# Shift filter as phase-by-channel contractions with keys turned on chip, gate sum from normalised rows, cross products ahead of the other spectral products

## The chip, the cores and the metric

The kernel runs on one core of one Trainium2 chip. The metric is the device time of one execution in microseconds (us), and a median over several executions is quoted. The profiled span is about 2 us shorter than the measured time.

The core has TensorE (PE, matrix products; PEld is its weight load), VectorE (DVE), ScalarE (ACT), GpSimd (POOL) and SyncE (SP, which issues DMAs). Each engine works through its own list of instructions in order; semaphores make one engine wait for another. A tile is a buffer in on-chip memory; PSUM tiles are here those that TensorE writes and ScalarE evicts.

## The reference, cut to what matters

```python
x = A_q                                             # 2048 rows of 640
g = sigmoid((x * gate_w).sum(-1, keepdims=True))    # one gate value per row
# branch A
k_shift = sum(k_pad[:, t:t+S, :] * shift_k[:, 3-t] for t in range(4))   # 4-tap causal filter per channel
kv = k_shift * v
y = irfft(rfft(kv, 2S) * rfft(ssm_k, 2S))[:S] + kv * ssm_D
a = q * y
# branch B
h = layernorm(x)
u = gelu(h^T @ w1 + b1);  b = (u @ w2 + b2)^T
out = g * a + (1 - g) * b
```

## The kernel before: the parts that matter

The long convolution is done as a discrete transform. TensorE multiplies by a 128x128 factor (`FTB`), VectorE combines the four phases ("mixing") and multiplies spectra, and TensorE transforms back. The 2048 rows come in four blocks of 512; partition i of a block holds rows 4i to 4i+3, one for each of four phases.

No order of instructions is written down. A list scheduler, run when the kernel is built, gives each engine its order from modelled durations. An operation with a smaller `prio` goes first among those that are ready. And where a later user of a PSUM tile (here GELU) has a hazard, the scheduler moves it onto the first matmul of that tile:

```python
                for d in deps:                      # hazards of the operation that reads the PSUM tile
                    if d.vt is not vt:
                        if d not in vt.first.deps:
                            vt.first.deps.add(d)    # ... now hold back the tile's first matmul
```

The first-layer matmuls of branch B have the last priority, so they fill what the rest leaves of TensorE:

```python
                mms(vt, items, prio=10 ** 6 + 4 * ft + hk, name="m1")
            g_ = act(GT[:, ft, :]..., two, ACT.Gelu_apprx_tanh, bias=..., vt=vt, prio=0, name="gelu")
```

The keys are transposed by DMA, 128 channels at a time. The filter multiplies strided columns of the transposed keys by diagonal matrices, seven matmuls for each group of 128 channels and each row block; ScalarE evicts, and VectorE multiplies by the values:

```python
                tt("DVE", DG[...], ident, shkf, ALU.mult)      # 20 diagonal matrices, once
        def kv(hk):
            # ... (cut)
                    for q in range(4):
                        items.append((s[512*b + 128*q : 512*b + 512], V(KT[h], base + q, [[4, 128]]), DG[:, db, 0:4 - q, :], ...))
                    for q in range(1, 4):
                        items.append((s[512*b : 512*b + 128*q], V(KT[h], base - 4 + q, [[4, 128]]), DG[:, db, 4 - q:4, :], ...))
                act(o, ..., ACT.Copy, vt=vt, name="kve")
            tt("DVE", o, kb[:, :, :], vi, ALU.mult, prio=0)    # kv = shifted keys times values
        for hk in range(2):
            kv(hk)                                             # first pair: vkv
        # first kv transform, mixing
        for hk in range(2, 4):
            kv(hk)                                             # second pair: kv
        # second kv transform, mixing
```

The gate sum is one VectorE instruction with accumulator for each of 16 row tiles, beside the row statistics. The spectral products come after both transforms:

```python
            stt("DVE", junk[1][:, :], xs, 1.0, gwb[:, :], ALU.mult, ALU.mult, acc=gpre[:, t:t + 1])
        # ... (cut)
        def y1(g):
            product(A1[g], A1[g], V0[g])
            product(V1[g], A0[g], V1[g])     # the cross product
            acc_dma(A1[g], V1[g])            # sum of both, by an accumulating DMA
```

## Time and profile before

| | before |
|---|---|
| median time | 203.06 us (202.98 to 203.24) |
| profiled span | 201.0 us |
| TensorE busy | 187.1 us, 93% |
| VectorE busy | 183.4 us, 91% |
| filter matmuls | 140 |

The timeline of TensorE before, 40 to 76 us: start, duration, engine, line, operation, tiles, count, and in brackets the idle just before with what ended it.

```profile
40.04 8.88 PE L293 MATMUL pp<-DG,KT 128*128 128x512 bf16 x70
...
51.44 1.25 PE L293 MATMUL pp<-X,ring 128*128 128x320 bf16 x8
52.53 9.39 PE L293 MATMUL pp<-vkv,FTB 128*128 128x320 bf16 x64
61.89 7.13 PE L293 MATMUL pp<-DG,KT 128*128 128x512 bf16 x56
68.86 3.42 PE L293 MATMUL pp<-X,ring 128*128 128x320 bf16 x24
72.12 0.43 PE L293 MATMUL pp<-kv,FTB 128*128 128x320 bf16 x2
73.91 2.08 PE L293 MATMUL pp<-kv,FTB 128*128 128x320 bf16 x14 [1.36 <-DVE kv L611]
```

Here `DG,KT` is the filter, `vkv,FTB` and `kv,FTB` are the first and second kv transform, and `X,ring` is the first layer, the filler. TensorE is nearly full while VectorE works towards the kv products; eight filler matmuls stand just ahead of the first transform.

The chain of waits of before, where it changes engine:

```profile
72.37 1.50 DVE kv L611
...
73.91 124.00 PE pp L293 x910
```

The last VectorE piece is the second product of the second pair.

### The profile page before, as it was taken

The numbers are of one execution on the slowest core, as the hardware profiler recorded it, in microseconds if no ns is written. First come the engines' busy times: TensorE is split into PE (matmuls) and PEld (weight loads), VectorE is DVE, ScalarE is ACT, GpSimd is POOL, SyncE is SP. The second block draws the span as 40 slices with busy tenths as digits, with TensorE's granted clock in tenths as the row PEclk, the third lists the DMA queues.
The fourth block names the chain that finished last, engine by engine and source line by source line (L and its number), as shares of the span: only waits on it lengthen the run. The fifth ranks groups of instructions, "written<-read, shape, count | busy, mean of one in ns | idle before, by whom it ended". The sixth has DMA issues, their size and how long they took to land.

```text
span 201.0 us, 3282 instructions
## 1 busy us (share of the span) xinstructions
PE 187.1 (93%) x1383; PEld 136.2 (68%) x1383; DVE 183.4 (91%) x204; ACT 102.9 (51%) x145; POOL 24.8 (12%) x24
## 2 busy tenths in 40 slices
PE   0769989999999979999999999999999999999993
PEld 0456656576656747777777777788888887688672
DVE  7799979998997999999999999999999982899672
ACT  4798899965698658841111221131313136631762
POOL 1002245403033060000000005003100000000000
PEclk9999999999999999999999999999999999999999
DMA  5999999999940000007501805995999900311033
GB/s 158 344 406 348 284 160 201 305 344 231 221 176 0 0 3 0 0 3 234 183 0 34 273 10 103 160 360 218 166 273 341 359 14 0 130 68 65 0 138 126
DMA packets 35226, 32.37 MB, mean 161 GB/s; under 512 B 15618, under 2 KB 32652, under 8 KB 35212
## 3 DMA queue, kind: packets, MB, share of 16 engines
q1 hardware_dynamic: 34080, 29.53, 49.2%
q0 software_dynamic: 1088, 2.62, 8.1%
q8 instruction: 11, 0.18, 0.4%
q14 instruction: 3, 0.02, 0.0%
q10 hardware_dynamic: 44, 0.01, 0.0%
HBM read 23.25 MB, written 2.62 MB: 129 GB/s over the span
## 4 chain that ended last, share of the span: by engine, by line
PE 62%; DVE 25%; POOL 5%; DMA 4%; issue 2%; SPq 1%; ACT 0%
PE pp L293 62%; DVE stats L825 5%; DVE junk L629 5%; DVE C L611 5%; DMA gwb<-in_gate_w_dram 4%; POOL vtmp L621 3%; DVE X L622 3%; DVE SS L611 3%; POOL rstd L611 2%; DVE kv L611 1%; DVE vkv L611 1%; DVE mv L827 1%; SPq L267 1%; ACT O L649 0%; DVE O L611 0%
## 5 line engine op out<-in xcount | busy, mean ns | idle before, releaser
L293 PE MATMUL pp<-X,ring 128*128 128x320 bf16 x384 | 53.6, 299 | 0.0
L293 PE MATMUL pp<-GT,W 128*128 128x320 bf16 x384 | 52.8, 299 | 0.0
L293 PEld LDWEIGHTS pp<-GT,W 128*128 128x128 bf16 x384 | 43.4, 113 | 8.9 <-issue 0.2
L611 DVE TENSOR_TENSOR C<-C 128x2560 bf16<-128x2560 bf16 (+1 forms) x28 | 49.0, 1769 | 0.3
L293 PEld LDWEIGHTS pp<-X,ring 128*128 128x128 bf16 x384 | 37.5, 98 | 14.5
L649 ACT ACTIVATE C<-pp 128x640 bf16<-128x640 f32 x64 | 39.3, 752 | 7.1 <-PE pp L293 7.0
L649 ACT ACTIVATE O<-pp,c,omg 128x640 bf16<-128x640 f32 (+1 forms) x17 | 14.5, 853 | 36.7 <-PE pp L293 36.7
L649 ACT ACTIVATE GT<-pp,cc 128x640 bf16<-128x640 f32 x12 | 9.5, 793 | 33.7 <-PE pp L293 33.7
L611 DVE TENSOR_TENSOR tm<-C,C 128x5120 bf16<-128x5120 bf16 x8 | 22.2, 2817 | 0.0
L293 PE MATMUL pp<-wT,FTB 128*128 128x320 bf16 x128 | 19.8, 314 | 0.0
L293 PE MATMUL pp<-DG,KT 128*128 128x256 bf16 (+3 forms) x140 | 18.1, 288 | 0.6 <-DMA KT<-in_A_k_dram 0.6
L611 DVE TENSOR_TENSOR C<-tm 128x2560 bf16<-128x2560 bf16 x12 | 17.4, 1484 | 0.1
L293 PEld LDWEIGHTS pp<-DG,KT 128*128 128x128 bf16 x140 | 13.1, 115 | 5.5 <-DMA KT<-in_A_k_dram 1.2
L293 PEld LDWEIGHTS pp<-wT,FTB 128*128 128x128 bf16 x128 | 11.8, 102 | 7.4 <-ACT C L649 2.5
L649 ACT ACTIVATE cgb<-pp,gg 128x640 bf16<-128x640 f32 x16 | 12.7, 793 | 5.7 <-PE pp L293 5.7
L293 PE MATMUL pp<-ident,ssm 128*128 128x128 bf16 x80 | 8.8, 266 | 6.9 <-DMA ssm<-in_A_ssm_k_dram 5.6
L825 DVE BATCH_NORM_STATS2 stats<-X 128x6 f32<-128x320 bf16 x32 | 13.7, 464 | 1.2 <-DMA X<-in_A_q_dram 1.2
L649 ACT ACTIVATE ksh<-pp 128x1024 bf16<-128x1024 f32 (+1 forms) x12 | 10.1, 879 | 8.2 <-PE pp L293 8.2
L293 PE MATMUL pp<-C,GTB 128*128 128x320 bf16 x96 | 13.6, 299 | 0.0
L629 DVE SCALAR_TENSOR_TENSOR junk<-X,gwb 128x640 bf16<-128x640 bf16 x16 | 12.9, 803 | 0.2 <-DMA gwb<-in_gate_w_dram 0.2
L262 POOL DMA_DIRECT2D C<-C x4 | 5.1, 1506 | 61.1 <-DVE C L611 61.1
L293 PEld LDWEIGHTS pp<-ident,ssm 128*128 128x128 bf16 x80 | 6.3, 128 | 9.2 <-DMA ssm<-in_A_ssm_k_dram 5.6
(49 smaller groups left out, 163.1 us busy)
## 6 DMA issues: line engine op xcount, KB each, us to landing
ring<-in_B_w_dram SPq DMA_DIRECT2D x12, 512.0 KB, 8.5
W<-in_B_w_dram SPq DMA_DIRECT2D x8, 768.0 KB, 7.8
ssm<-in_A_ssm_k_dram SPq DMA_DIRECT2D x4, 640.0 KB, 9.0
X<-in_A_q_dram SPq DMA_DIRECT2D x4, 640.0 KB, 9.2
C<-C POOLq DMA_DIRECT2D x4, 640.0 KB, 9.1
out_dram<-O SPq DMA_DIRECT2D x7, 320.0 KB, 2.4
vkv<-in_A_v_dram SPq DMA_DIRECT2D x2, 640.0 KB, 5.0
v<-in_A_v_dram SPq DMA_DIRECT2D x2, 640.0 KB, 6.3
```

Source lines behind the costliest of these rows:

```text
L262: ins = engobj.dma_start(out_ap, in_ap, accum_op=ALU.add, max_dma_last_dim=2560)
L267: ins = engobj.dma_start(out_ap, in_ap)
L293: ins = self.nc.tensor.matmul(ps_ap, lhsT=lhsT, rhs=rhs, start=start, stop=stop, skip_group_check=True)
L611: return SC.add(eng, d, lambda s: T.op(eng, lambda e: e.tensor_tensor(o, a, b, op), [a, b], [o]), [a, b], [o], prio=prio, name="tt")
L621: return e.tensor_scalar(o, a, s1, None, op0=op0)
L622: return e.tensor_scalar(o, a, s1, s2, op0=op0, op1=op1)
L629: eng, lambda e: e.scalar_tensor_tensor(out=o, in0=a, scalar=sc, in1=b, op0=op0, op1=op1, accum_out=acc),
L649: return T.op("ACT", lambda e: e.activation(o, src, func, **kw), rr + [src], ww)
L825: SC.add("DVE", 0.46, (lambda o, i: lambda s: T.op("DVE", lambda e: e.bn_stats(o, i), [i], [o]))(o, i), [i], [o])
L827: SC.add("DVE", 0.2, (lambda o, i: lambda s: T.op("DVE", lambda e: e.bn_aggr(o, i), [i], [o]))(o, i), [i], [o])
```

## The change

The intent is to relieve TensorE and VectorE in the first 74 us.

- **Filter.** VectorE permutes natural key rows (`kn` to `kp`), and a DMA turns them so that a column holds 4 phases by 32 channels. One matmul contracts those 128 values at once; a second one, shifted by a column, adds the taps that reach into the four rows before. 140 matmuls become 160 narrower ones. The filter matrix `KF` is built by two GpSimd products.
- **Gate.** With the row normalised already, the sum is that of the normalised row times `gate_w`, scaled back by the row's deviation, plus the mean times the sum of `gate_w`. VectorE multiplies later (8 wider products), ScalarE sums, and GpSimd combines 16 numbers per partition.
- **Cross product.** It goes ahead of the other products, in halves, so that it can start before the second mixing.

```diff
+        kn = [alloc(f"kn{i}", [128, 4, D], BF16, at=base_of(ring[1]) + 5120 * i) for i in range(2)]
+        kp = [alloc("kp0", ..., at=base_of(ring[1]) + 10240), alloc("kp1", [128, NG, 128], BF16, at=base_of(GT))]
...
-        def kT_load(h, db):
-            dma(KT[h][:, db, 16:1040], A_k[...], transpose=True, chain=True)
+        def k_turn(hk):
+            o, i = kp[hk % 2], kn[hk % 2]
+            ... tensor_copy(ov, iv) on VectorE
+            dma(KT[hk // 2][:, :, c0:c0 + 128], o[:, :, :], transpose=True, chain=True)
...
-            stt("DVE", junk[1][:, :], xs, 1.0, gwb[:, :], ALU.mult, ALU.mult, acc=gpre[:, t:t + 1])
...
-                tt("DVE", DG[...], ident, shkf, ALU.mult, mode=1)
+                for g0 in (0, 10):
+                    tt("POOL", KF[:, g0:g0 + 10, :, :], cw taps, m32 mask, ALU.mult)
+                for hk in range(2):
+                    k_turn(hk)
...
+                    items.append((s[128*b : 128*b + 128], KT[h][:, g, c0:c0 + 128], KF[:, g, 0:4, :], True, False))
+                    items.append((s[128*b : 128*b + 96], KT[h][:, g, c0 - 1:c0 + 127], KF[:, g, 4:7, :], False, True))
...
+            if ft in (1, 3, 5, 7):
+                    tt("DVE", gb[:, :, :], X[...], gwb, ALU.mult)
+                        act(junk[:, :], gb[:, b, :], ACT.Copy, acc=gacc[:, t:t + 1], name="gsum")
+        tt("POOL", gth, vtmp, rstd);  tt("POOL", gth, gth, gacc)
+        ts("POOL", gpre, mv mean, gws);  tt("POOL", gpre, gpre, gth)
+        act(gth[:, :], gpre[:, :], ACT.Tanh, scale=0.5)
...
         def y1(g):
             product(A1[g], A1[g], V0[g])
-            product(V1[g], A0[g], V1[g])
...
+        cross(0)
+        cross(1)
         y1(0)
```

## The prediction

> **What bounds it now.** The chain of waits falls in two. From 9 to 73.9 us it is almost all VectorE (statistics, gate sums, mixings, kv products), with some GpSimd; from 73.9 to 197.9 us it is TensorE alone, 910 matmuls (busy by stretch: 123.98 of 124.10 us). So the time is T, the end of the second kv product, plus about 127 us that only fewer matmuls after T shorten. Before T, TensorE is busy 60 of 65 us, partly with filler (48 first-layer matmuls).
>
> **What changes (groups and timeline of before).**
> - Filter: 140 matmuls, 17.4 us of TensorE, become 160 of 128 or 96 columns. The 128-column transposes, each with new weights, follow one another every 55 ns or so (five in 0.31 us of weight loads), so I estimate 8.5 to 9 us. ScalarE then limits: a 1024-column eviction takes 0.92 us, so a quarter of the filter needs 2.3 us. All of it lies before T.
> - VectorE loses 16 gate products (0.80 us each with the accumulator read: 12.9 us) and the 2.77 us diagonal build. It gains eight 1280-column products (0.74 us each, after T, where it has room) and four key permutations, estimated 0.85 us each, before T. Net before T: about 12 us less.
> - GpSimd gains two 128x2240 products for the filter matrix. The Trainium skill, "GPSIMD Engine Reference", section 3.1, gives 4497 ns for 2048 elements; scaled, an estimate of 4.9 us each. No run yet shows it.
>
> **Critical path.** Adding up the changed order with durations of before (the same sum puts before at 201 us of span, T at 73.6): the filter ends near 43 us, against 52.5; but the first transform of kv waits for VectorE, which reaches the kv products only at 47 to 54 us. No filler stands there, so TensorE idles 4 to 8 us: most of its saved 9 us. The value-mixing operations now stand ahead of the second pair of kv products. The second filter-matrix product comes when VectorE runs two-input operations. The skill, "SBUF — State Buffer", section "Who interferes with whom", says these and a GpSimd read exclude each other; before agrees in part (a GpSimd scaling of 4 elements took 2.69 us beside one long VectorE operation, 0.24 us elsewhere). If VectorE loses about 5 us there, directly or by waiting for the row scale queued behind it, T is about 74 us; if not, 70 us. After T there are 8 matmuls more (1.1 us).
>
> **Time.** Span 198.7 to 205; the measured time is 2 us above the span. I predict 202.3 us, range 197.5 to 207: faster by over 2% 0.2, within 2% 0.67, slower by over 2% 0.13. The large TensorE saving buys nearly nothing.
>
> **What would show each step.**
> - TensorE busy about 178 us instead of 187, with one idle of 4 us or more before the first kv transform, ended by a VectorE product.
> - Filter matmuls about 9 us in all, paced by ScalarE evictions.
> - VectorE at about 178 us busy; about 5 us lost near 20 to 40 us, beside the second GpSimd filter-matrix product.
> - The chain: VectorE until about 74 us, then TensorE unbroken.
>
> **What would make it wrong.** Permutations at half the assumed rate (T about 2.5 us later), or GpSimd products of 7 us (+4 us): slower. GpSimd running freely beside VectorE: T near 70, about 200.5 us. The gate's GpSimd steps, queued between long VectorE operations, could hold the Tanh and stall ScalarE and TensorE near 105 us; I expect 3 to 4 us, hidden by two open output buffers.

## More of the kernel before

The page of the profile of before: the first row gives busy us, share of the span and instruction count for each engine. The PE and PEclk rows cut the span in 40 slices of 5 us (busy share and granted clock in tenths). The last row says which engine the chain that ended last runs through.

```profile
PE 187.1 (93%) x1383; PEld 136.2 (68%) x1383; DVE 183.4 (91%) x204; ACT 102.9 (51%) x145; POOL 24.8 (12%) x24
...
PE   0769989999999979999999999999999999999993
...
PEclk9999999999999999999999999999999999999999
...
PE 62%; DVE 25%; POOL 5%; DMA 4%; issue 2%; SPq 1%; ACT 0%
```

Groups of before: busy us, mean ns of one, then the idle of the engine before them.

```profile
L293 PE MATMUL pp<-vkv,FTB 128*128 128x320 bf16 x64 | 9.4, 301 | 0.0
L629 DVE SCALAR_TENSOR_TENSOR junk<-X,gwb 128x640 bf16<-128x640 bf16 x16 | 12.9, 803 | 0.2 <-DMA gwb<-in_gate_w_dram 0.2
L622 DVE TENSOR_SCALAR X<-X,mv,rstd 128x640 bf16<-128x640 bf16 x16 | 6.1, 442 | 3.3 <-POOL rstd L611 3.3
```

## The result, and the profile after

| | before | after |
|---|---|---|
| median time | 203.06 us | 205.34 us (205.13 to 207.21) |
| profiled span | 201.0 us | 203.6 us |
| TensorE busy | 187.1 us | 180.8 us |
| VectorE busy | 183.4 us | 182.0 us |
| ScalarE busy | 102.9 us | 116.1 us |
| GpSimd busy | 24.8 us | 48.8 us |

The ratio of the times is 1.0132, 95% interval 1.0093 to 1.0172: a small loss within 2%. Ratios here are the mean time of one kernel's runs over that of the other's of the same rounds, so not quite the ratio of the medians quoted. TensorE works 6.3 us less, and the kernel takes 2.3 us more.

The page of the profile of after, the rows that answer to those of before:

```profile
PE 180.8 (89%) x1403; PEld 131.5 (65%) x1403; DVE 182.0 (89%) x193; ACT 116.1 (57%) x183; POOL 48.8 (24%) x33
...
PE   0769989951599999999999799999999999999993
...
PEclk9999999996589999999999999999999999999999
...
PE 67%; DVE 17%; POOL 6%; DMA 3%; issue 2%; ACT 2%; SPq 0%; DVEq 0%; POOLq 0%
```

Two things are new: a hole of TensorE in the slices at 40 to 55 us (the digits 5, 1, 5), and a granted clock that falls just behind its start. The timeline of TensorE after:

```profile
39.06 4.33 PE L293 MATMUL pp<-KF,KT 128*128 128x128 bf16 x80
50.17 0.69 PE L293 MATMUL pp<-vkv,FTB 128*128 128x320 bf16 x2 [6.78 <-DVE vkv L617]
52.95 10.00 PE L293 MATMUL pp<-vkv,FTB 128*128 128x320 bf16 x54 [2.09 <-DVE vkv L617]
62.78 1.25 PE L293 MATMUL pp<-X,ring 128*128 128x320 bf16 x8
...
64.95 4.34 PE L293 MATMUL pp<-KF,KT 128*128 128x128 bf16 x80
69.13 4.51 PE L293 MATMUL pp<-X,ring 128*128 128x320 bf16 x32
...
113.13 7.09 PE L293 MATMUL pp<-X,ring 128*128 128x320 bf16 x51 [1.46 <-ACT GT L655]
```

The filter does shrink, to 4.33 and 4.34 us. But the first transform still cannot run in earnest before 52.95 us, because its second VectorE product ends then (in before it ended at 52.74 us). All that the filter saved ahead of that is now idle, 6.78 and 2.09 us. No `X,ring` filler stands in the hole: the first 8 such matmuls of after come at 62.78 us, where before had 24 by 52.5 us (16 of them ahead of 40 us).

The busy stretches of TensorE in after: stretch, its length, busy us (and instructions), granted clock, DMA share, GB/s.

```profile
44.00:50.00 6.00, 0.00 (x0) 0.78 0.96 398
50.00:53.00 3.00, 0.74 (x3) 0.50 0.39 80
53.00:58.00 5.00, 5.00 (x21) 0.54 1.10 207
58.00:63.00 5.00, 5.00 (x37) 1.00 0.94 278
```

So the first 5 us of the transform run at about half clock. In before, the clock was 1.00 over these stretches. Groups of after:

```profile
L293 PE MATMUL pp<-vkv,FTB 128*128 128x320 bf16 x64 | 11.9, 351 | 8.9 <-DVE vkv L617 8.9
L628 DVE TENSOR_SCALAR X<-X,mv,rstd 128x640 bf16<-128x640 bf16 x16 | 9.6, 667 | 3.6 <-POOL rstd L617 3.6
L627 POOL TENSOR_SCALAR gpre<-mv,gws 128x16 f32<-128x16 f32 x1 | 14.0, 14028 | 17.0 <-ACT junk L655 17.0
L655 ACT ACTIVATE gth<-gpre 128x16 f32<-128x16 f32 x1 | 0.2, 217 | 6.7 <-POOL gpre L617 6.7
```

The mean of the row normalisation rose from 442 to 667 ns with no change to the instruction itself. The mean hides that a single one of the 16 did it. Their median is 441 ns in after (440 ns in before), but one took 4.07 us, beside the second GpSimd product for the filter matrix:

```profile
20.33 4.07 DVE L628 TENSOR_SCALAR X<-X,mv,rstd 128x640 bf16<-128x640 bf16 x1
...
20.19 4.03 POOL L617 TENSOR_TENSOR KF<-cw,m 128x2240 bf16<-128x2240 bf16 x1
```

A GpSimd operation on 16 elements took 14.0 us, and a later one (`gth`, 5.67 us) made ScalarE wait 6.7 us before the Tanh. The chain of waits of after, where it changes engine:

```profile
51.49 1.41 DVE vkv L617
...
52.95 14.14 PE pp L293 x110
...
105.53 5.68 POOL gth L617
...
113.13 87.39 PE pp L293 x640
```

The hand-over from VectorE to TensorE is now the first pair of kv products at 52.95 us, not the second pair at 74 us. Behind it the chain is broken once, by the gate.

From these traces a first account, counted from where the first transform starts (52.5 us in before, 52.95 us for all but its first two matmuls in after):

- second half of the filter: 7.13 to 4.34 us, a gain of 2.8 us
- 24 filler matmuls that had been done by then, still to do: an estimate of 24 x 0.136 = 3.3 us (0.136 us is the spacing of first-layer matmuls)
- low clock in the transform: 54 matmuls took 10.00 us, while 64 took 9.39 us before, so 2.1 us more
- the gate's stall of 1.46 us, which stands against the old wait of 1.36 us for the second pair

The sum, with the 0.4 us of the later start, is 3.1 us, against 2.6 us measured between the spans. It is an account from two traces; which terms are causes had to be tried. One caution for all the trials: most edits also change the order that the list scheduler gives to the other engines, so a run often tests more than its edit. Only e9 against e7 keeps every order.

**Theory A.** VectorE fixes the start of the first transform. What the change saves before that is worth something only if first-layer matmuls can fill the hole. They cannot, because the new buffer `kp1` lies in the memory of the first four GELU output tiles. By the scheduler's rule above, GELU's write hazard holds back the first matmul of every such tile until the last keys have been turned. **Rival B**: the low clock is the main loss. **Rival C**: VectorE is slower, by the lock with GpSimd's products (the normalisation of 4.07 us), and that is the main loss. **Rival D**: the gate's stall.

### The profile page after: what moved, and what is told of

Its sections match the earlier page's. It is cut to its first block, busy times and chain, and to the rows that moved or that the text cites. A ratio compares the mean times of both kernels' runs of the same rounds, so it can differ in the third digit from the quotient of the medians.

```text
span 203.6 us, 3356 instructions
## 1 busy us (share of the span) xinstructions
PE 180.8 (89%) x1403; PEld 131.5 (65%) x1403; DVE 182.0 (89%) x193; ACT 116.1 (57%) x183; POOL 48.8 (24%) x33
## 4 chain that ended last, share of the span: by engine, by line
PE 67%; DVE 17%; POOL 6%; DMA 3%; issue 2%; ACT 2%; SPq 0%; DVEq 0%; POOLq 0%
PE pp L293 67%; DVE X L628 4%; DVE stats L842 4%; DMA X<-in_A_q_dram 3%; DVE C L617 3%; POOL gth L617 3%; DVE SS L617 3%; POOL KF L617 2%; DVE kp L724 1%; DVE vkv L617 1%; POOL rstd L617 1%; ACT junk L655 1%; DVE mv L844 1%; SPq L267 0%; POOL gpre L617 0%
## 5 line engine op out<-in xcount | busy, mean ns | idle before, releaser
L655 ACT ACTIVATE C<-pp 128x640 bf16<-128x640 f32 x64 | 40.0, 794 | 12.6 <-PE pp L293 12.1
L617 DVE TENSOR_TENSOR tm<-C,C 128x2560 bf16<-128x2560 bf16 (+1 forms) x12 | 22.7, 1926 | 0.0
L293 PE MATMUL pp<-vkv,FTB 128*128 128x320 bf16 x64 | 11.9, 351 | 8.9 <-DVE vkv L617 8.9
L627 POOL TENSOR_SCALAR gpre<-mv,gws 128x16 f32<-128x16 f32 x1 | 14.0, 14028 | 17.0 <-ACT junk L655 17.0
L617 DVE TENSOR_TENSOR C<-tm 128x1280 bf16<-128x1280 bf16 (+1 forms) x16 | 17.9, 1153 | 0.2
L293 PEld LDWEIGHTS pp<-wT,FTB 128*128 128x128 bf16 x128 | 10.8, 101 | 9.5 <-ACT C L655 4.4
L293 PEld LDWEIGHTS pp<-vkv,FTB 128*128 128x128 bf16 x64 | 6.6, 111 | 13.9 <-issue 6.9
L628 DVE TENSOR_SCALAR X<-X,mv,rstd 128x640 bf16<-128x640 bf16 x16 | 9.6, 667 | 3.6 <-POOL rstd L617 3.6
L655 ACT ACTIVATE junk<-gq 128x640 bf16<-128x640 bf16 x16 | 11.8, 736 | 0.5
```

Source lines behind the costliest of these rows:

```text
L293: ins = self.nc.tensor.matmul(ps_ap, lhsT=lhsT, rhs=rhs, start=start, stop=stop, skip_group_check=True)
L617: return SC.add(eng, d, lambda s: T.op(eng, lambda e: e.tensor_tensor(o, a, b, op), [a, b], [o]), [a, b], [o], prio=prio, name="tt")
L627: return e.tensor_scalar(o, a, s1, None, op0=op0)
L628: return e.tensor_scalar(o, a, s1, s2, op0=op0, op1=op1)
L655: return T.op("ACT", lambda e: e.activation(o, src, func, **kw), rr + [src], ww)
```

## The experiments

Times of before were 202.98 to 203.17 us. All results were correct.

### e1: turned keys kept out of GELU's memory

```diff
-        kn = [... at=base_of(ring[1]) + 5120 * i) for i in range(2)]
-        kp = [alloc("kp0", at=base_of(ring[1]) + 10240), alloc("kp1", at=base_of(GT))]
+        kn = [... at=base_of(ring[1]) + 5120 * b) for i, b in enumerate((0, 1, 1, 0))]
+        kp = [... at=base_of(ring[1]) + 5120 * b) for i, b in enumerate((2, 0, 2, 1))]
```

The buffers of the four key blocks rotate through three places inside the second weight buffer, which is free at that time.

> The changed kernel, with the buffers of the turned keys moved out of the memory of the first four GELU output tiles into the second weight buffer (the key buffers rotate there). Nothing else is edited; the scheduler may then place first-layer matmuls early. Theory A (the filter's saved array time was lost because TensorE had nothing else it was allowed to do while VectorE prepared the kv products): 48 or more first-layer matmuls stand before the first kv transform, TensorE's idle time between 38 and 54 us falls from 8.9 us to under 4 us, the clock stays full, and the time falls by 4 to 6 us, to 199.5 to 201.5 us. Rival B (only the slowed clock after the idle stretch costs time): about 2 us less, 203.2 us. Rival C (the gate's Tanh stall at 111 us and the new key path cost the time): no change, 205 us.

Measured: 199.59 us, ratio 0.9823 (0.9809 to 0.9838), 5.75 us under after. The timeline of TensorE in e1:

```profile
48.39 3.43 PE L293 MATMUL pp<-X,ring 128*128 128x320 bf16 x24
51.66 0.43 PE L293 MATMUL pp<-vkv,FTB 128*128 128x320 bf16 x2
52.96 0.99 PE L293 MATMUL pp<-vkv,FTB 128*128 128x320 bf16 x6 [0.86 <-DVE vkv L617]
```

The second product still arrives at 52.96 us, but now 24 filler matmuls stand ahead of the transform, the clock stays at 1.00 and the transform's matmuls take 300 ns. This fits theory A, but it also mends the clock, and it might have other effects. Runs e5, e6 and e9 part these.

### e2: useless matmuls in the hole

44 matmuls of 320 columns, whose result nobody reads, between filter and first transform of after.

```diff
         for hk in range(2):
             kv(hk)
+        vt = _VT("cv")
+        mms(vt, [(chk(0), KT[0][...], KF[...320 columns], b == 0, b == 43) for b in range(44)], name="warm")
```

> The changed kernel with 44 useless 320-column matmuls between the filter of the first half and the first kv transform, so that TensorE is busy but gains nothing. The output is right. Theory A: the hole still gives no useful work, so at most the clock's part comes back: the first kv transform runs at full clock (mean matmul near 300 ns instead of 351 ns) and the time falls by 1.5 to 2.5 us, to about 203 us, far from what the useful filler of the first run gives. Rival B (clock is all): the same as the first run. Rival C: no change, 205 us.

Measured: 204.73 us, ratio 1.009 (1.0068 to 1.0111), 0.6 us under after; 1.5 to 2.5 were expected. The useless work ended at 49.5 us, and TensorE idled 0.57 and then 2.35 us with two matmuls between. Over 53 to 58 us the clock was 0.66 (0.54 in after) and the transform's matmuls took 334 ns. So the experiment was too weak to test the clock, and rival B as the main cause was not favoured by it. e9 repeats it with the second wait closed.

### e3: filter matrix built by VectorE

```diff
-                    tt("POOL", KF[:, g0:g0 + 10, :, :], ...
+                    tt("DVE", KF[:, g0:g0 + 10, :, :], ...
```

> The changed kernel with the two filter-matrix products on VectorE instead of GpSimd (about 1.25 us each there). Theory A with the port conflict: the row scale no longer waits 1.7 us behind the first product, and the eight normalisations take 3.0 us instead of 6.6 us; less 2.5 us for the products themselves, the second kv product of the first half ends about 2.5 us earlier, near 50.4 us, and the time falls by 2 to 3 us, to 202.5 to 203.5 us. If the normalisations were slow for another reason they stay at 6.6 us, and the time rises by about 1 us, to 206 to 207 us.

Measured: 202.58 us, ratio 0.9973 (0.9958 to 0.9987), 2.8 us under after. VectorE pays 2.45 us for each of the two products, about twice what had been assumed. The long normalisation is gone (the longest takes 447 ns), and the transform's second input is there at 50.79 us instead of 52.95 us. But the second does not follow from the first. VectorE's order changed as well:

```profile
45.81 2.81 DVE L617 TENSOR_TENSOR C<-C 128x5120 bf16<-128x5120 bf16 x1
```

is the mixing that stands just ahead of the first pair's products in after; in e3 it stands behind them:

```profile
49.25 1.48 DVE L617 TENSOR_TENSOR vkv<-ksh,vkv 128x2560 bf16<-128x2560 bf16 x1
...
51.51 2.77 DVE L617 TENSOR_TENSOR C<-C 128x5120 bf16<-128x5120 bf16 x1
```

One key permutation moved behind the second product too. VectorE came to this place 1.3 us later than in after (47.12 against 45.81 us), so what it gained by the missing lock was more than spent on the two products and on waits for row scales (0.65 and 1.25 us). The earlier start of 2.2 us is the new order. Another 1.3 us of e3's gain stands at the gate, where TensorE's stall is 0.20 us instead of 1.46 us. So rival C is not shown by this run: the lock is real (3.6 us on one instruction), but no run tried what it costs in time with the order kept. The hole of TensorE stays (5.90 and 1.35 us) and the clock in it stays low.

### e4: e1 and e3 together

> Both edits: key buffers out of the GELU tiles, filter-matrix products on VectorE. Theory A: the two gains come from the same wait, but the filler then covers it, so they add only in part: 197.5 to 200.5 us, 1 to 2 us below the first run. Rival B: about 203 us. If what is left is the Tanh stall of 1.5 us near 110 us, it is still seen in the waits of ScalarE.

Measured: 198.6 us (198.26 to 198.79), ratio 0.9774 (0.976 to 0.9789): faster than before by 2.3%. With filler available, e3's edit is worth 1.0 us, not 2.8 us. That TensorE no longer stands idle for all of VectorE's delay fits this but was not tried by itself; the order on VectorE differs here too.

### e5: e1 with the filler withheld

Memory and waits of e1, but the scheduler may start no first-layer matmul before the last matmul of the first transform.

```diff
-                mms(vt, items, prio=10 ** 6 + 4 * ft + hk, name="m1")
+                m_ = mms(vt, items, prio=10 ** 6 + 4 * ft + hk, name="m1")
+                m_.after.add(fw2)     # fw2: last matmul of the first kv transform
```

> The kernel of run e1 (turned keys rotated inside the weights' ring, GELU's memory left free), but the scheduler is told to start no first-layer matmul before the last matmul of the first kv transform. Nothing else differs; memory and waits are those of e1. Theory A (what e1 gained is only that first-layer matmuls may fill the hole again): about 24 first-layer matmuls move behind the transform, the idle of TensorE at 43 to 53 us is 7 to 10 us again with 24 or more first-layer matmuls gone from it, and the time is that of the changed kernel, 204.0 to 206.0. Rival (e1 gained by shorter waits of the key turns or by another order of VectorE): the time stays at 199.5 to 201.5.

Measured: 203.08 us (202.69 to 203.82), ratio 1.0002 (0.9978 to 1.0026). It loses 3.5 us of the 5.75 us of e1, and it is 0.9 us below the range that theory A named.

```profile
50.06 0.69 PE L293 MATMUL pp<-vkv,FTB 128*128 128x320 bf16 x2 [7.25 <-DVE vkv L617]
52.11 10.99 PE L293 MATMUL pp<-vkv,FTB 128*128 128x320 bf16 x62 [1.36 <-DVE vkv L617]
```

The hole is back with the clock at 0.50 to 0.66, as expected. Two differences from after account for the miss: the second product came 0.84 us earlier (52.11 against 52.95 us), and there is no stall at the gate. GpSimd was not faster there: its last gate step ended at 112.05 us in both runs. ScalarE's order differs: in e5 one more GELU stands ahead of the Tanh,

```profile
106.43 0.79 ACT L655 ACTIVATE GT<-pp,cc 128x640 bf16<-128x640 f32 x1 [1.97 <-PE pp L293]
112.08 0.22 ACT L655 ACTIVATE gth<-gpre 128x16 f32<-128x16 f32 x1 [4.85 <-POOL gpre L617]
```

where in after the last GELU ahead of the Tanh starts at 103.01 us and the next only at 112.21 us. So withholding the filler costs 3.5 us with memory unchanged (the low clock behind the hole included), and the rest of e1's gain lies elsewhere.

### e6: the kernel before with its filler withheld

The same edit on before.

> The kernel before, with the same order to the scheduler: no first-layer matmul before the last matmul of the first kv transform. Theory A (the kernel before owes part of its time to the 24 to 48 first-layer matmuls that it runs in VectorE's shadow): 16 to 24 matmuls of 0.136 us that ran before about 52 us come behind it, 2.2 to 3.3 us, and part may still fit the later wait for the second pair: 204.5 to 207.0. Rival (filler is worth nothing because VectorE sets the pace until 74 us): within 0.7 us of the kernel before, 202.4 to 203.8.

Measured: 205.65 us (205.05 to 206.1), ratio 1.0122 (1.0102 to 1.0143): before loses 2.5 us in this way, with the clock at 1.00 throughout. So before owes its time in part to filler in VectorE's shadow, and the clock plays no part in this 2.5 us. The order moved here as well: 14 filter matmuls of the second pair went ahead of the first transform, where they waited for keys (0.48 and 0.39 us), and the transform began at 54.04 us instead of 52.53 us. So 2.5 us is not the price of the filler alone. It is about what after loses in all, which by itself proves nothing.

### e7: Tanh later

```diff
-        act(gth[:, :], gpre[:, :], ACT.Tanh, scale=0.5)
+        act(gth[:, :], gpre[:, :], ACT.Tanh, scale=0.5).after.add(gelus[10])
```

> The changed kernel, with the gate's Tanh put behind the eleventh GELU in ScalarE's order instead of the tenth's neighbourhood, so that GpSimd has more time for its 16-element steps. Theory A (the stall of TensorE of 1.46 us at 112 us is lost for good, because everything behind it on TensorE is unbroken): stall gone or below 0.4 us, 203.3 to 204.6. Rival (the stall is given back later, at the second layer or the inverse transform): 205.0 to 205.8. If the starved steps merely end later still, the stall moves and stays, 205 or more.

Measured: 203.85 us (203.15 to 204.44), ratio 1.0045 (1.0025 to 1.0065), 1.5 us under after, the size of the stall in the trace. The stall is gone (the first layer runs unbroken from 86.94 us on, past 113 us). Rival D is a real part of 1.5 us. The range of this run is wide against that difference, and the clock in its hole was a little better too (0.69 over 53 to 58 us, against 0.54).

### e8: the kernel before with the new gate alone

```diff
-            stt("DVE", junk[1][:, :], xs, 1.0, gwb[:, :], ALU.mult, ALU.mult, acc=gpre[:, t:t + 1])
+            # products of 1280 columns on VectorE and sums on ScalarE beside the first layer,
+            # the 16-element steps on GpSimd, then the Tanh, all as in the changed kernel
```

> The kernel before with the new gate alone (the 16 gate products of 0.81 us leave VectorE's early part; old filter, old cross product). The prediction's picture (VectorE sets the pace until 74 us, so about 13 us less of it brings the second pair of kv products earlier): 199 to 201.5. Theory A (TensorE's order is full from about 53 us on, and VectorE's relief before that only makes it wait elsewhere; the wait of 1.36 us for the second pair may go, and GpSimd's starved steps may cost 1 to 2 us at the Tanh): 202.0 to 205.0.

Measured: 204.02 us (203.88 to 204.14), ratio 1.0043 (1.0028 to 1.0058). Taking 12.9 us of VectorE work out of the first 74 us gains nothing; 0.9 us is lost. The first transform starts no earlier: its second product begins at 52.43 us, since in VectorE's order it stands behind a normalisation that waits for GpSimd's row scale until 52.06 us, and the filter on TensorE ends only at 51.8 us. The second transform starts at 77.49 us without a wait for its products. So the prediction's picture does not hold: less VectorE work ahead of 74 us brought neither pair forward, and the chain of this run hands over to TensorE with the first pair (53.97 us, then TensorE unbroken from 59.10 us).

### e9: the hole filled completely, Tanh later

e7 and 64 useless matmuls; the order of everything else is that of e7.

> Run e7 (the changed kernel with the later Tanh) and 64 useless matmuls of 320 columns between the filter and the first kv transform, 8.7 us, which bridge both waits for VectorE (run e2's 44 left the second wait of 2.35 us open, and the granted clock still was 0.66 at 53 to 58 us). The order of all other instructions on every engine is that of e7. Theory (the low clock after the hole costs about what the transform's matmuls lengthen, 1.3 us in e7 against 9.4 us at full clock, and no more): granted clock 1.00 throughout, the transform's matmuls 300 ns, the time 1.0 to 1.7 us under e7, about 202.2 to 202.9. Rival (the low clock is repaid elsewhere or is harmless): as e7, 203.5 to 204.2. If the clock were the main part of the loss, 200.5 or less.

Measured: 202.71 us (202.64 to 202.83), ratio 0.9991 (0.9974 to 1.0007), 1.1 us under e7, and steadier. The group in e9:

```profile
L293 PE MATMUL pp<-vkv,FTB 128*128 128x320 bf16 x64 | 9.6, 300 | 0.4 <-DVE vkv L617 0.4
```

The clock costs 1.1 us here, where e7's transform took 1.3 us more than at full clock; it is not repaid elsewhere, and it is not the main loss. e9 does in the hole work that nobody needs, e1 does first-layer work there. That difference, 202.71 to 199.59, is 3.1 us. That it is close to the 3.3 us estimated for 24 matmuls is chance: when the second half of the filter begins, e1 has 80 first-layer matmuls behind it and e9 has 8. TensorE ends its last matmul 5.0 us earlier in e1 (192.74 against 197.73 us), but in e1 no filler is left beside the last inverse transform, and 4.9 us follow it until the span ends, against 3.2 us in e9.

### e10: the changed kernel with the old cross product

```diff
         def y1(g):
             product(A1[g], A1[g], V0[g])
+            product(V1[g], A0[g], V1[g])
...
-        cross(0)
-        cross(1)
```

> The changed kernel with the old cross product (behind the first-layer stage, at full width, no product ahead of the second transform); filter and gate as changed. Theory (VectorE is idle or not binding between 88 us and 160 us, and TensorE's order there is unbroken): the same as the changed kernel within 0.7 us, 204.6 to 206.0. Rival (the cross product ahead of time is a gain of its own, because the inverse transform can start sooner): 206.5 or more.

Measured: 203.09 us (202.78 to 203.97), ratio 1.0015 (0.999 to 1.0039), 2.25 us under after. This contradicts both expectations; the old cross product is better here. TensorE has no stall at the gate, and the reason stands in the timelines of VectorE and GpSimd. In after:

```profile
108.24 2.88 DVE L617 TENSOR_TENSOR tm<-C,C 128x2560 bf16<-128x2560 bf16 x2
111.16 1.58 DVE L617 TENSOR_TENSOR C<-tm 128x1280 bf16<-128x1280 bf16 x2
...
105.53 5.67 POOL L617 TENSOR_TENSOR gth<-gth,gacc 128x16 f32<-128x16 f32 x1 [17.31 <-ACT junk L655]
```

and in e10:

```profile
102.77 5.56 DVE L617 TENSOR_TENSOR tm<-C,C 128x5120 bf16<-128x5120 bf16 x2
108.36 2.92 DVE L617 TENSOR_TENSOR C<-tm 128x2560 bf16<-128x2560 bf16 x2
...
105.67 2.73 POOL L617 TENSOR_TENSOR gth<-gth,gacc 128x16 f32<-128x16 f32 x1 [18.61 <-ACT junk L655]
```

VectorE's two-input operations overlap by some hundredths of a microsecond, except where one waits for the result of the one before. In after such a gap stands at 111.12 to 111.16 us (108.24 + 2.88), and GpSimd's step ends at 111.20 us. In e10 it stands at 108.33 to 108.36 us, and the step ends at 108.40 us. GpSimd gets through in VectorE's first gap, and the new cross product's order puts that gap 2.8 us later. By these times it ends the stall, 1.5 us. The traces' spans differ by just that (203.6 and 202.1 us); the other 0.75 us of the medians stays open, with a range of 2.1 us for after's own executions.

### e11: e4 with the last product begun earlier

```diff
         product(A0[0], A0[0], V0[0])
+        tt("DVE", P2(T0), P2(A0[1]), P2(V0[1]), ALU.mult)
+        tt("DVE", P2(T1), P2(A0[1]), P2(V0[1], True), ALU.mult)
         Z1 = invmix(A1[0], A1[1], C3a, None, None)
```

> Run e4 (turned keys inside the ring, filter matrix by VectorE) with the last product of the second half begun earlier: its two multiplications come ahead of the sums that wait for the accumulating DMA, where VectorE idled 2.69 us in e4. Theory (with the first part mended, the next limit is VectorE's last stretch: TensorE waited 1.48 us for it at 182 us in e4): that wait of TensorE is gone or under 0.5 us, 196.8 to 198.0. Rival (the first-half inverse is bound elsewhere): 198.2 to 198.9 as e4.

Measured: 198.18 us (198.11 to 198.47), ratio 0.9769 (0.9754 to 0.9783). The theory fell: TensorE's wait of 1.48 us at 182.88 us stayed. VectorE's wait for the DMA shrank from 2.69 to 1.67 us, and one for ScalarE at 167 us grew from 0.32 to 1.47 us. The 0.4 us under e4 is not explained by the trace, and the executions of both overlap (198.26 to 198.79 in e4), so a gain over e4 is not shown. By its median this is the fastest kernel, 2.3% under before.

### e12: e4 with the old cross product

> Run e4 (turned keys inside the ring, filter matrix by VectorE) with the old cross product. Theory (in e10 the old cross product gained only because the new one's smaller back-to-back VectorE operations had kept GpSimd's two last gate steps waiting, 5.67 us against 2.74 us, and with them the Tanh; in e4 the Tanh stalls TensorE not at all, so nothing is left to gain): 198.2 to 199.4, as e4 or up to 0.8 us over it, because VectorE has no product behind it when its last stretch begins. Rival (the new cross product costs 2 us in itself, by its smaller operations on VectorE or its wait of 2.6 us for the accumulating DMA): 196.0 to 197.2.

Measured: 199.76 us (198.94 to 200.66), ratio 0.9824 (0.9781 to 0.9867), 1.2 us over e4 by the medians; 0.4 us above what was expected. The interval reaches past 2%, so it is unclear whether it is faster than before by more than 2%. The four executions fall in two pairs: 198.94 and 199.02 us with a mean clock of 0.995 and 0.996, and 200.49 and 200.66 us with 0.989 and 0.987. The trace is of one of the slow pair. The old cross product gains nothing where the gate does not stall. In this trace VectorE has more left at the end:

```profile
183.27 6.20 PE L293 MATMUL pp<-C,GTB 128*128 128x320 bf16 x32 [2.22 <-DVE C L617]
```

TensorE waits 2.22 us there (1.48 us in e4), the granted clock over 184 to 190 us is 0.72 (1.00 in e4), and the 32 matmuls take 6.20 us instead of 4.57. The faster pair lies only 0.2 us above e4's slowest execution (198.79 us). So the third part of the change is worth perhaps half a microsecond once its side effect on the gate is gone; the rest of the 1.2 us goes with the low clock of two executions.

## Why the prediction was right or wrong

It was right that the large saving on TensorE would buy nearly nothing, and the time fell in its range; it was 3.0 us too low. The range of 9.5 us was wide, and part of the hit is luck: the point T on which the sum was built came out near the forecast without being what bound the time. Point by point:

- **TensorE's saving and the hole.** Predicted: 8.5 to 9 us for the filter, an idle of 4 to 8 us ended by a VectorE product, TensorE busy about 178 us. Measured: 8.67 us, 6.78 + 2.09 us ended by `vkv`, 180.8 us busy. The mechanism was right. The 2.8 us too much of busy time is for the larger part the transform at low clock, whose group rose from 9.4 to 11.9 us. The pace of the filter was wrong: it was not set by ScalarE's evictions, as 80 matmuls ran unbroken in 4.33 us.
- **VectorE and GpSimd.** Predicted: about 5 us lost at 20 to 40 us beside the second filter-matrix product, or by waiting for the row scale behind it. Measured at 17.5 to 25.8 us: a wait of 1.73 us for the row scale, and eight normalisations in 6.57 us against 3.0 us (twice the 1.51 us that four took in before), together 5.3 us. The size was right, but the victim was not a two-input operation, as predicted: it was one normalisation, held for 4.07 us. The products took 3.99 us each, not 4.9 us. The Trainium skill, "SBUF — State Buffer", section "Who interferes with whom", says that an operation like it can contend as well, and that the engine which comes second is blocked for the whole instruction; 4.07 us beside a product of 4.03 us agrees. VectorE's busy time, predicted at 178 us, was 182.0 us, and 3.6 us of this is that one instruction.
- **The step that failed** is the time as T plus a rest, with T the end of the second kv product near 74 us: "the chain: VectorE until about 74 us, then TensorE unbroken". The chain of after hands over at 52.95 us with the first pair; the second pair ended about 72.6 us and its transform began at 73.47 us, behind filler, without a wait. So T plus 127 us, with the predicted 1.1 us for eight more matmuls, would be 200.7 us, and the span was 203.6 us. Of the 2.9 us between, 1.46 us is the gate's stall and 0.9 us the start behind T, because TensorE still had filler to do; the rest is small. TensorE without a break from 52.95 us to the gate was the path, not VectorE until 74 us. e8 shows the same from the other side: 12.9 us less of VectorE work before T brought no gain (the old filter, which ends at 51.8 us there, is a second reason). The wait of 1.36 us at 73.91 us in before had only been the last one of a chain.
- **Terms that the sum lacked.** Counted instead from the path that bound, TensorE from 52.95 us on, two terms are new. The clock: 2.1 us in the trace of after; the part that was tried costs 1.1 us (e9 against e7). The gate's stall: predicted as 3 to 4 us held and hidden, measured 6.7 us held and 1.46 us exposed, 1.5 us by e7. Together 2.6 to 3.6 us, about the 3.0 us by which the prediction was low.
- **Where the gain went.** From after to e1 the time falls by 5.75 us: 1.5 us of gate stall (e7), 1.1 us of clock (e9) and 3.1 us of first-layer work moved into the hole (e1 against e9) sum to 5.7 us. The runs form a line from after over e7 and e9 to e1, so this sum is the whole by construction and no check; what they show is how it divides. e1 keeps the old place of the Tanh, with a stall of 0.30 us, and has a new wait of 1.07 us at 162 us, so its 3.1 us is what is left after those. That no filler stood in the hole was foreseen in one sentence, but not that this was an accident of memory: moving the buffers of the turned keys, 5 KB per partition each, undid it.

What stays open: why e10 gained 0.75 us more than the stall, whether e11 gained anything over e4, what the lock on VectorE costs with the order kept, and what the changed kernel would do with the old gate alone.

## What to carry to other kernels

Work saved on an engine that waits later for another one is only worth what can be moved into the hole; before removing work, ask which filler will stand there and what its own hazards are. When a buffer is laid over memory that another stage will write, look at which instruction inherits that hazard, as it may not be the one that writes. Small operations on GpSimd, off the critical path by size, can end up on it when VectorE runs two-input operations without a gap. When a scheduler orders the program, compare the order of every engine before you credit an edit with a gain: in e3 and e5 a moved instruction explained what had looked like a faster one.

## What the Trainium skill lacked or had wrong

- "SBUF — State Buffer", "Who interferes with whom", says that whoever issues first holds the shared ports for the whole instruction. It lacks that GpSimd can be starved over many VectorE instructions: an operation on 16 elements took 14.0 us in after and 38.5 us in e9. Each ended 0.2 us after VectorE's next gap began, one of 0.59 us at 88.02 us in after and one of 0.03 us at 110.38 us in e9. The steps of 5.67 us (after) and 2.73 us (e10) ended within 0.1 us of gaps of 0.04 and 0.03 us. The same kind of step took 0.2 to 0.8 us where it met no such stretch.
- "TensorE: Matmul & The Clock Gate", Part 1, puts the fall of the clock after an idle window of about 3.4 us. The hole of 6.78 us agrees (0.50 granted at 50 to 53 us). But shorter waits lowered it too: 0.57 and 2.35 us, two matmuls apart, were followed by 0.66 at 53 to 58 us in e2, and one wait of 2.22 us by 0.72 at 184 to 190 us in e12, while neither 1.48 us in e4 nor 2.03 us near 10 us in before did anything. No fixed length comes out of these runs.
- "TensorE: Matmul & The Clock Gate", Part 2, "Back-to-back issue gap", gives about 81 ns as the sustained spacing of 128-column matmuls with a weight load each. Here 80 matmuls, half of 128 and half of 96 columns, each with new weights, took 4.33 us, 54 ns each.
- "GPSIMD Engine Reference", section 3.1, gives 4497 ns for a two-input addition of 2048 fp32 elements. Scaled by elements that is an estimate of 4.9 us for 2240; in bf16 with broadcast inputs it took 3.94 and 4.03 us.
